# Retention front on one NeuronCore: eight units before the first layer, two tiles by turns on each weight, GpSimd given decays and low parts

## The chip, the cores and the metric

The kernel runs on one core of a Trainium2 chip. The metric is device microseconds of one execution; the median of three runs before the change is 1460.3 us (1460.2 to 1460.72).

## The reference

Retention with decay per head, then two gated or maximum feed-forward layers, all in float32:

```python
scores = scale * np.matmul(q, k.transpose(0, 1, 3, 2))          # 8 x 8 heads, 576 x 64
Dmat = np.where(rel >= 0, gamma[:, None, None] ** rel[None, :, :], 0.0)
attn = np.matmul(scores * Dmat[None, :, :, :], v)
x = attn.transpose(0, 2, 1, 3).reshape(B * S, H * D)            # 4608 x 512
h = np.maximum(np.maximum(x @ w1, x @ w2), x @ w3)              # 512 -> 768
x = h @ w_out                                                   # 768 -> 512
h = x @ w_in                                                    # 512 -> 2048
out = (h * np.clip(h + 3.0, 0.0, 6.0) / 6.0) @ w_out2           # 2048 -> 512
```

## The kernel before, in words

**Numbers.** TensorE multiplies in the fp32r type. Every operand of the feed-forward layers is kept as a high part (a cast on ScalarE) and a low part (the value minus the high part), and a product is three matmuls: high by high (L462), high by low (L463), low by high (L464). The weights come as float64 bits and are turned into floats on the core.

**A weight.** `Weights.step` is one conversion step for a 128x512 weight tile. On VectorE it runs L113 and L114 for the weight that begins, L132 and L134 for the one that joins and L154 (the low part) for the one that ends; on ScalarE L121, L124 and the cast L148; on GpSimd one product, L136. A weight passes through three steps. `fetch` loads the next weight tile (512 KB of int64) on SP's queue; three such tiles fit.

**A unit.** One unit is one batch and a pair of heads, 576 positions in nine chunks of 64. Its raw data is 1152 KB, loaded in two halves of 576 KB, first the two value parts (V), then the two others (Z). `prepare` multiplies the keys by decays (nine ScalarE instructions, L348). `keys` issues the sums of key times value (L356) and the scores (L277) on TensorE. `copied`, `mask` and `join` bring them back (ScalarE L368, VectorE L395 and L385). `values_mm` multiplies them (L313), `values_rest` scales the result (VectorE L411), and `finish` makes the high part of x on ScalarE (L326) and the low part on VectorE (L327). The ninth chunk has small instructions of its own (L405, L418).

**The order.** All is written out by hand (`manual_schedule`), and each engine runs its instructions in that order. The first eight units (batches 0 and 1, class `Summed`) stand in the front. In the first four the weight steps lie between the units' parts; in the last four there is also a `block` in each of two places. A block is `up` (12 matmuls of 512 columns) or `down` (12 as well) of tile 0 or 1. Eight blocks of tile 0 lie in the front so, and the list `plan` holds the next 39 of the two tiles. From `plan`'s end on, units of the next tile are computed between blocks (`visit`, `rest`, `ready`), and wherever TensorE has a block after that it has little else to wait for.

**Rooms.** Raw data of units sits in two pools of three tiles (`raw`, `rooms`): the seventh unit loaded takes the tile of the first. SP, the queue that issues nearly all transfers, uses eight semaphores in turn, so that a ninth transfer is not issued before the first has landed, and a transfer that has to wait for a tile holds back all that stand behind it in SP's order.

Of the kernel before, what the change touches and what calls it, by code (L numbers as in the profile page):

```python
# [7 lines left out]
F32 = mybir.dt.float32  # L8
# [8 lines left out]
P = 128  # L17
# [20 lines left out]
def retention_moe_moe2(ctx: ExitStack, tc, raw, w_a, w_b, factors, masks, out):  # L38
# [22 lines left out]
    xe_d = dram.tile([P, KM, TB], F32, name="xed")  # L61
    wq_d = [dram.tile([P, 7, 2, 2 * P], F32, name=f"wqd{j}") for j in range(F2 // 2)]
# [157 lines left out]
    order_a.insert(8, order_a.pop(6))  # L220
# [35 lines left out]
    xs, low = {}, []  # L256
    banks = [ps_at.tile([P, 512], F32, name=f"at{n}") for n in range(2)]

    class Unit:
# [63 lines left out]
        def finish(self, queue=late):  # L323
            b, hp, y = self.b, self.hp, self.y
            hi, lo = xs[b][:, 0, hp, :], xs[b][:, 1, hp, :]
            nc.scalar.copy(hi, y[:, :TB])  # L326
            queue.append(lambda: nc.vector.tensor_tensor(out=lo, in0=y[:, :TB], in1=f32(hi), op=ALU.subtract))  # L327
            late.append(lambda: nc.sync.dma_start(out=xe_d[:, hp, b * C:(b + 1) * C], in_=y[:, TB:]))
# [11 lines left out]
    class Summed(Unit):  # L340
# [3 lines left out]
        def prepare(self):  # L344
            h = (NC - 1) // 2
            for c in [*range(h, NC), *range(h)]:
                k = self.part(1, c, None, VS1)
                nc.scalar.mul(k, k, kdec_sb[:, self.hp, c:c + 1])  # L348

        def keys(self):  # L350
            h = (NC - 1) // 2
            for n, c in enumerate([*range(h, 2 * h), *range(h)]):
# [8 lines left out]
                self.scores(n, self.ps[0], n * C)  # L361
# [7 lines left out]

        def carry(self):  # L370
            t, h = raws[self.i], (NC - 1) // 2
            for e in (1, 0):
                own, other = halves[e], halves[1 - e]
                nc.tensor.matmul(
                    self.ps[1][other, h * C:].rearrange("p (n d) -> p n d", d=D), lhsT=same_sb[other, :],
                    rhs=self.part(e, h, VS0, VS1)[other, None, :].to_broadcast([D, h, D]),
                    start=False, stop=True, skip_group_check=True)
            self.copied(h)
# [19 lines left out]
        def values_mm(self):  # L398
            self.scores(NC - 1, self.ps[0], 0)
            self.values(range(NC - 1), self.ps[1])  # L400
            t = raws[self.i]
            for e in range(2):
                own, other = halves[e], halves[1 - e]
                z0 = (Z0, Z1)[e] + (NC - 1) * C
                nc.vector.scalar_tensor_tensor(  # L405
                    out=t[own, z0:z0 + C], in0=self.ps[0][other, :C], scalar=powers_sb[other, self.hp, 0, NC - 1:],
                    in1=mask_sb[other, self.hp], op0=ALU.mult, op1=ALU.mult)
# [546 lines left out]
```

## Time and profile before

| | |
|---|---|
| median of three runs | 1460.3 us |
| profiled execution: time, span | 1460.34 us, 1458.5 us |
| TensorE busy | 1442.5 us, 99% of the span |
| VectorE, ScalarE, GpSimd busy | 894.9, 458.2, 152.4 us |
| mean granted TensorE clock | 0.999 |
| HBM read, written | 174.42 MB, 42.99 MB |

Lines L12 are those of the kernel file. PE is TensorE, DVE VectorE, ACT ScalarE, POOL GpSimd, SP the queue that issues the transfers. A float32 matmul (L277, L313, L356) shows twice in the trace, once for each of its passes. The time is 1.84 us more than the span; that part lies around the execution and is taken as it is.

### The profile page before, as it was taken

What the parts mean: (1) busy time and instruction counts of PE and PEld (TensorE: products, weight loads), DVE (VectorE), ACT (ScalarE), POOL (GpSimd) and SP (SyncE); (2) the same over time, 40 slices, a digit from 0 to 9 for tenths busy, and PEclk for the clock granted to TensorE, in tenths of its full rate; (3) what the DMA queues carried; (4) which work ended last, traced back from release to release, by engine and by line L of the source; (5) the groups of instructions that cost most, each with busy time, mean ns of one, the idle gap of its engine ahead of it and who ended that gap; (6) DMA issues with size and microseconds to landing.
All of it is one profiled execution on the core that took longest, in us unless ns stands there. A gap on an engine that the chain in (4) does not pass through costs nothing.

```text
span 1458.5 us, 24565 instructions
## 1 busy us (share of the span) xinstructions
PE 1442.5 (99%) x9760; PEld 1248.3 (86%) x9760; DVE 894.9 (61%) x1867; ACT 458.2 (31%) x882; POOL 152.4 (10%) x116
## 2 busy tenths in 40 slices
PE   8999999999999999999999999999999999999998
PEld 7788888888888888888898899898898898898997
DVE  6997778777778752214446646555654655566544
ACT  7653233434343311112222322232232222223222
POOL 3332013333333300000000000000000000000000
PEclk9999999999999999999999999999999999999999
DMA  9543345656565501064643363364445436444431
GB/s 347 170 129 107 130 142 193 230 204 233 195 221 197 195 13 53 7 213 141 224 125 114 113 213 116 101 223 117 116 148 177 116 87 238 116 115 168 116 101 44
DMA packets 94499, 219.03 MB, mean 150 GB/s; under 512 B 14128, under 2 KB 17328, under 8 KB 94384
## 3 DMA queue, kind: packets, MB, share of 16 engines
q1 hardware_dynamic: 94016, 216.96, 45.3%
q8 instruction: 78, 1.28, 0.3%
q10 hardware_dynamic: 368, 0.48, 0.1%
q14 instruction: 37, 0.30, 0.1%
HBM read 174.42 MB, written 42.99 MB: 149 GB/s over the span
## 4 chain that ended last, share of the span: by engine, by line
PE 91%; DVE 7%; ACT 1%; DMA 1%; issue 1%; SPq 0%; ACTq 0%; DVEq 0%
PE mm L462 18%; PE mm L464 17%; PE mm L463 17%; PE o L795 5%; PE o L796 5%; PE o L794 5%; PE o L462 3%; PE o L463 3%; PE o L464 3%; PE p L796 3%; PE p L795 3%; PE p L794 3%; PE mm L313 2%; PE at L277 1%; DVE xf L685 1%
## 5 line engine op out<-in xcount | busy, mean ns | idle before, releaser
L53 ACT CAST gp<-g 128x384 fp32r<-128x384 f32 x192 | 98.6, 513 | 336.9 <-DVE g L751 331.9
L462 PE MATMUL mm<-x,w 128*128 128x512 f32 x468 | 185.2, 396 | 0.1
L464 PE MATMUL mm<-x,w 128*128 128x512 f32 x468 | 182.6, 390 | 0.0
L463 PE MATMUL mm<-x,w 128*128 128x512 f32 x468 | 182.5, 390 | 0.0
L54 DVE TENSOR_TENSOR gp<-g,gp 128x384 fp32r<-128x384 f32 x192 | 107.2, 558 | 112.2 <-ACT gp L53 112.2
L758 DVE TENSOR_TENSOR cc<-mm,c 128x384 f32<-128x384 f32 x142 | 78.7, 554 | 136.9 <-PE mm L464 95.4
L479 DVE TENSOR_TENSOR t<-mm,t 128x512 f32<-128x512 f32 x108 | 74.1, 686 | 135.4 <-PE mm L464 135.3
L795 PE MATMUL o<-w,gp 128*128 128x512 f32 x384 | 151.3, 394 | 0.0
L796 PE MATMUL o<-w,gp 128*128 128x512 f32 x384 | 150.7, 392 | 0.0
L794 PE MATMUL o<-w,gp 128*128 128x512 f32 x384 | 150.2, 391 | 0.0
L462 PE MATMUL mm<-T,wq 128*128 128x384 f32 x382 | 129.8, 340 | 0.9 <-ACT c L763 0.2
L763 ACT COPY c<-mm 128x384 f32<-128x384 f32 x143 | 68.5, 479 | 196.7 <-PE mm L464 196.7
L464 PE MATMUL mm<-T,wq 128*128 128x384 f32 x382 | 129.0, 338 | 0.0
L463 PE MATMUL mm<-T,wq 128*128 128x384 f32 x382 | 128.7, 337 | 0.0
L136 POOL TENSOR_TENSOR wf<-wf,wp 128x512 f32<-128x512 f32 x56 | 82.6, 1475 | 342.9 <-DVE wp L134 329.7
L462 PEld LDWEIGHTS mm<-x,w 128*128 128x128 f32 x468 | 87.9, 188 | 20.9 <-DVE wp L113 1.4
L464 PEld LDWEIGHTS mm<-x,w 128*128 128x128 f32 x468 | 87.9, 188 | 18.6
L463 PEld LDWEIGHTS mm<-x,w 128*128 128x128 f32 x468 | 88.0, 188 | 17.7
L53 ACT CAST h<-t 128x512 fp32r<-128x512 f32 x54 | 33.6, 622 | 204.6 <-DVE t L479 199.1
L462 PE MATMUL mm<-B,wq 128*128 128x384 f32 x286 | 96.5, 337 | 0.0
L464 PE MATMUL mm<-B,wq 128*128 128x384 f32 x286 | 96.4, 337 | 0.0
L463 PE MATMUL mm<-B,wq 128*128 128x384 f32 x286 | 96.2, 336 | 0.0
(177 smaller groups left out, 2923.1 us busy)
## 6 DMA issues: line engine op xcount, KB each, us to landing
wq<-wqd SPq DMA_DIRECT2D x336, 256.0 KB, 3.1
raw<-in_raw SPq DMA_DIRECT2D x55, 576.0 KB, 5.4
ws<-in_w_b SPq DMA_DIRECT2D x32, 512.0 KB, 4.6
ws<-in_w_a SPq DMA_DIRECT2D x24, 512.0 KB, 3.5
wqd<-y SPq DMA_DIRECT2D x24, 512.0 KB, 2.7
x2d<-y SPq DMA_DIRECT2D x18, 512.0 KB, 3.3
wod<-y SPq DMA_DIRECT2D x16, 512.0 KB, 3.0
w<-wod SPq DMA_DIRECT2D x16, 512.0 KB, 4.4
```

The costliest lines, as they stand in the source:

```text
L53: nc.scalar.copy(hi, full)
L54: late.append(lambda: nc.vector.tensor_tensor(out=lo, in0=full, in1=f32(hi), op=ALU.subtract))
L136: nc.gpsimd.tensor_tensor(out=frac, in0=frac, in1=f32(power), op=ALU.mult)
L462: nc.tensor.matmul(ps, lhsT=wh, rhs=xh, start=first, stop=False, skip_group_check=read)
L463: nc.tensor.matmul(ps, lhsT=wh, rhs=xl, start=False, stop=False, skip_group_check=read)
L464: nc.tensor.matmul(ps, lhsT=wl, rhs=xh, start=False, stop=last, skip_group_check=read)
L479: nc.vector.tensor_tensor(out=tmp[t, f], in0=ps, in1=tmp[t, f], op=ALU.max)
L758: nc.vector.tensor_tensor(out=c, in0=a, in1=b, op=ALU.add)
L763: nc.scalar.copy(c, ps)
L794: nc.tensor.matmul(outs[s], lhsT=gh, rhs=wo[f][:, 0, :], start=start, stop=False)
L795: nc.tensor.matmul(outs[s], lhsT=gh, rhs=wo[f][:, 1, :], start=False, stop=False)
L796: nc.tensor.matmul(outs[s], lhsT=gl, rhs=wo[f][:, 0, :], start=False, stop=stop)
```

## The change

- `prepare`: of units 2 to 7 one GpSimd instruction over all nine chunks (128x576). Units 0 and 1 keep ScalarE for five chunks and use one VectorE instruction for four.
- `finish`: the low part of x is made on GpSimd for seven of the eight front units, on VectorE for the last.
- The ninth chunk of the eight units is not computed in the front. `put_end` stores its four inputs (128 KB in pieces of 256 bytes) to HBM; class `Ends` loads all of them once (1 MB), and computes scores and values for the eight units behind two blocks of `plan`.
- The front holds the eight units, three conversion steps (behind units 2, 3 and 4) and one block, (0, 0, 0), behind unit 6. `carry` is gone: all units use `join`.
- `plan` holds the up blocks of tiles 0 and 1 by turns on each weight from the first weight on.
- Unit 5 is loaded before the table fills; weight tiles are fetched at other places, and unit 6 is loaded behind `put_end` of unit 0, unit 7 behind `put_end` of units 1 and 2.

```diff
-        def finish(self, queue=late):
+        def finish(self, eng=None):
             hi, lo = xs[b][:, 0, hp, :], xs[b][:, 1, hp, :]
             nc.scalar.copy(hi, y[:, :TB])
+            def rest(eng):
+                eng.tensor_tensor(out=lo, in0=y[:, :TB], in1=f32(hi), op=ALU.subtract)
+            if eng is not None:
+                rest(eng)
...
+            def scaled(eng, n):
+                eng.tensor_tensor(out=k[:, :n], in0=k[:, :n], in1=kdec_sb[:, self.hp, :n, None].to_broadcast([P, n, C]),
+                                  op=ALU.mult)
+            if self.i > 1:
+                scaled(nc.gpsimd, NC)
+                return
...
         def values_mm(self):
-            self.scores(NC - 1, self.ps[0], 0)
             self.values(range(NC - 1), self.ps[1])
...
+            self.finish(nc.vector if self.i == 2 * HP - 1 else nc.gpsimd)
+        def put_end(self):
+            t = raws[self.i].rearrange("p (k s) -> p k s", s=S)
+            nc.sync.dma_start(out=ends_d[:, self.b, self.hp], in_=t[:, :, TB:])
+    class Ends:
+        def load(self):
+            t = at.tile([P, RAW], F32, tag="raw", bufs=3, name="raw")[:, :2 * HP * 4 * C]
+            nc.sync.dma_start(out=t, in_=ends_d.rearrange("p b h k c -> p (b h k c)"))
...
+        def scores(self):
+            for b, hp in units[:2 * HP]:
+                for e in range(2):
+                    nc.tensor.matmul(ps[other, b, hp], lhsT=self.t[other, b, hp, 1 - e],
+                                     rhs=self.t[other, b, hp, e], start=True, stop=True)
...
         for i, u in enumerate(us):
             u.values_mm()
             if two:
                 two.keys()
                 two.copied(0)
             if three:
                 three.prepare()
             u.values_rest()
             if two:
                 two.mask()
+                two.join()
+            u.put_end()
+            if i == 0:
+                load_raw(6)
+                wa.fetch(1)
+            if i == 2:
+                load_raw(7, room())
+            if 1 < i < 5:
+                wa.step()
+            if i == 2 * HP - 2:
+                block(0, 0, 0)
+        ends = Ends()
+        load_raw(8)
+        load_raw(9)
+        ends.load()
...
-        plan = [(1, 0, j) for j in range(3)] + [(0, 0), (0, 2, 2)] + [(1, 1, j) for j in range(3)] + [(0, 1)]
+        plan = []
+        for f in range(F1 - 1):
             for j in range(3):
                 plan += [(0, f, j), (1, f, j)]
+            if f:
+                plan.append((0, f - 1))
```

SP's queue in the front. `raw` and `room` are units' data (from the top units 0, 1, 2, 3, 4, 5, 6, 7), `ws` weight tiles, `xed` and `endsd` the HBM tiles of the ninth chunks. Before:

```order
L238 DMA room_150<-in_raw 128x1152 x2
L100 DMA ws_153<-in_w_a 128x512
L238 DMA raw_395<-in_raw 128x1152 x2
L328 DMA xed_75<-yr_385 128x64
L100 DMA ws_428<-in_w_a 128x512
L238 DMA raw_483<-in_raw 128x1152 x2
L328 DMA xed_75<-yr_473 128x64
L100 DMA ws_518<-in_w_a 128x512
L238 DMA room_572<-in_raw 128x1152 x2
```

After, at the same place:

```order
L238 DMA room_149<-in_raw 128x1152 x2
L101 DMA ws_152<-in_w_a 128x512
L238 DMA raw_154<-in_raw 128x1152 x2
L419 DMA endsd_76<-raw_134 128x4x64
L238 DMA raw_364<-in_raw 128x1152 x2
L101 DMA ws_367<-in_w_a 128x512
L419 DMA endsd_76<-raw_138 128x4x64
L419 DMA endsd_76<-room_141 128x4x64
L238 DMA room_489<-in_raw 128x1152 x2
```

Unit 6 (`raw_364`) takes the tile of unit 0 (`raw_134`), which the store just ahead of it reads, and unit 7 (`room_489`) takes the tile of unit 2 (`room_141`), again read by the store just ahead; before, nothing read those tiles so late. One weight tile fewer stands ahead of unit 5.

VectorE at the end of the front: `yr` is a unit's scaled result, `x` its low part, `t` the maximum of two up blocks. Before, the last unit's end:

```order
L411 TENSOR_TENSOR yr_1046<-at1_122,w_126 128x512
L418 SCALAR_TENSOR_TENSOR yr_1046<-at0_121,factors_sb_119,masks_sb_120 128x64
L327 TENSOR_TENSOR x_166<-yr_751,x_166 128x512
L327 TENSOR_TENSOR x_166<-yr_875,x_166 128x512
L327 TENSOR_TENSOR x_166<-yr_971,x_166 128x512
L327 TENSOR_TENSOR x_166<-yr_1046,x_166 128x512
L479 TENSOR_TENSOR t_1061<-mm_1072,t_1061 128x512
```

After (`w_772` is the second weight):

```order
L413 TENSOR_TENSOR yr_754<-at1_123,w_127 128x512
L329 TENSOR_TENSOR x_168<-yr_754,x_168 128x512
L114 TENSOR_SCALAR wp_774<-ws_567 128x512
L115 TENSOR_SCALAR wf_775<-ws_567 128x512
L133 SCALAR_TENSOR_TENSOR wf_632<-ws_367,wf_632 128x512
L135 SCALAR_TENSOR_TENSOR wp_631<-ws_367,wp_631 128x512
L155 TENSOR_TENSOR w_772<-wf_559,w_772 128x512
```

The low part of the second weight is now made behind the last unit's end and four instructions of a conversion step; before, eight weights were ready at this place.

## Rows read from the trace of the kernel before

**Rows 1.** The page: busy time, share of the span and instructions of each engine.

```profile
PE 1442.5 (99%) x9760; PEld 1248.3 (86%) x9760; DVE 894.9 (61%) x1867; ACT 458.2 (31%) x882; POOL 152.4 (10%) x116
```

**Rows 2.** Stretch 70 to 140: length, busy of each engine, granted clock, DMA, GB/s.

```profile
70.00:140.00 70.00, 70.00 (x310) 57.99 (x309) 62.54 (x100) 34.25 (x59) 23.84 (x15) 1.00 0.38 123
```

**Rows 3.** TensorE's waits from 60 to 160: total, times, longest.

```profile
PE at L313 <- DVE room L405: 0.5, 1, 0.5
```

**Rows 4.** TensorE in order of time: start, duration, line, tiles, shape; 61 to 68.

```profile
61.98 0.39 PE L464 MATMUL mm<-x,w 128*128 128x512 f32 x1
...
62.56 1.15 PE L313 MATMUL at<-room 128*64 128x64 f32 x32
63.64 0.50 PE L462 MATMUL mm<-x,w 128*128 128x512 f32 x1
63.98 0.40 PE L463 MATMUL mm<-x,w 128*128 128x512 f32 x1
...
67.38 0.50 PE L462 MATMUL mm<-x,w 128*128 128x512 f32 x1
```

**Rows 5.** TensorE, the last matmul of the 29th block from 67.38 on.

```profile
146.19 0.39 PE L464 MATMUL mm<-x,v 128*128 128x512 f32 x1
```

**Rows 6.** DMA issues from 15.0 to 19.7: count, KB, us to landing.

```profile
raw<-in_raw SPq DMA_DIRECT2D x1, 576.0 KB, 11.4
xed<-yr SPq DMA_DIRECT2D x1, 32.0 KB, 6.9
```

**Rows 7.** SP's queue in order of time: start, issuing time, transfer.

```profile
13.76 1.61 SPq L238 DMA_DIRECT2D raw<-in_raw  x2
19.66 0.33 SPq L328 DMA_DIRECT2D xed<-yr  x1
...
28.41 1.57 SPq L238 DMA_DIRECT2D room<-in_raw  x2
```

**Rows 8.** DMA issues from 51.8 to 52.3 (issued at 51.87 and 52.25).

```profile
raw<-in_raw SPq DMA_DIRECT2D x1, 576.0 KB, 4.5
ws<-in_w_a SPq DMA_DIRECT2D x1, 512.0 KB, 3.5
```

**Rows 9.** GpSimd in order of time: the table fills, and one product beside VectorE.

```profile
5.72 8.06 POOL L335 TENSOR_TENSOR w<-masks_sb,factors_sb 128x512 f32<-128x512 f32 x8 [5.28 <-DMA masks_sb<-in_masks]
...
28.03 1.67 POOL L136 TENSOR_TENSOR wf<-wf,wp 128x512 f32<-128x512 f32 x1 [4.41 <-DVE wp L134]
```

**Rows 10.** TensorE, a unit's keys and scores: its first and its last row.

```profile
13.85 0.43 PE L356 MATMUL o<-room 64*64 64x256 f32 x2
...
15.96 0.28 PE L356 MATMUL o<-room 64*64 64x64 f32 x4
```

**Rows 11.** TensorE, one up block's first matmul and what follows its last.

```profile
37.01 0.50 PE L462 MATMUL mm<-x,w 128*128 128x512 f32 x1
...
39.96 0.34 PE L313 MATMUL at<-room 128*64 128x64 f32 x4
```

**Rows 12.** TensorE, one of three idle times with no releaser (the others 1.03, 1.13).

```profile
19.85 0.43 PE L356 MATMUL mm<-room 64*64 64x256 f32 x2 [1.33 <-issue]
```

**Rows 13.** TensorE's last matmul.

```profile
1452.13 0.39 PE L796 MATMUL p<-w,gp 128*128 128x512 f32 x1
```

**Rows 14.** Stretch 1455 to 1456, columns as in rows 2.

```profile
1455.00:1456.00 1.00, 0.00 (x0) 0.00 (x0) 0.00 (x0) 0.00 (x0) 0.00 (x0) 0.50 0.95 248
```

**Rows 15.** VectorE in order of time: a scaled result, four low parts, a conversion step.

```profile
28.46 0.68 DVE L411 TENSOR_TENSOR yr<-o,w 128x512 f32<-128x512 f32 x1
...
33.88 2.49 DVE L327 TENSOR_TENSOR x<-yr,x 128x512 fp32r<-128x512 f32 x4
36.28 0.42 DVE L113 TENSOR_SCALAR wp<-ws 128x512 uint32<-128x512 uint32 x1
...
38.16 0.69 DVE L154 TENSOR_TENSOR w<-wf,w 128x512 fp32r<-128x512 f32 x1
```

**Rows 16.** ScalarE, the cast to a unit's high part.

```profile
19.60 0.61 ACT L326 CAST x<-yr 128x512 fp32r<-128x512 f32 x1
```

More of the change, by code (lines that the diff above doesn't have):

```diff
@@ L345, in prepare, with keys @@
             h = (NC - 1) // 2
[L346 to L350, printed above, removed]
+            k = raws[self.i][:, VS1:VS0].rearrange("p (c s) -> p c s", s=C)
+            def scaled(eng, n):
[4 more added lines that the diff above has]
+                return
+            for c in range(h, NC):
+                nc.scalar.mul(k[:, c], k[:, c], kdec_sb[:, self.hp, c:c + 1])
+            scaled(nc.vector, h)
+        def keys(self, apart=False):
             h = (NC - 1) // 2
@@ L360, in keys @@
                         start=(c == h), stop=(c == h - 1), skip_group_check=True)
-                self.scores(n, self.ps[0], n * C)
+                if not apart:
+                    self.scores(n, self.ps[0], n * C)
+            if apart:
+                for n in range(2 * h):
+                    self.scores(n, self.ps[0], n * C)
         def copied(self, c):
@@ L368, in copied @@
                 nc.scalar.copy(t[other, v0:v0 + n], self.ps[1][other, c * C:c * C + n])
[L370 to L378, printed above, removed]
         def join(self):
@@ L518, in retention_moe_moe2 @@
         load_raw(2, room())
-        wa.fetch(1)
         load_raw(3, room())
@@ L523, in retention_moe_moe2 @@
         wa.fetch(1)
+        load_raw(5)
         nc.vector.memset(rebias, -896.0)
@@ L536, in retention_moe_moe2 @@
         us[0].prepare()
-        us[0].keys()
+        us[0].keys(apart=True)
+        us[0].copied(0)
         us[1].prepare()
-        us[0].copied(0)
         us[0].mask()
@@ L558, in block @@
                 up(t, f, j)
-        early = [(0, f, j) for f in range(3) for j in range(3)][:8]
         for i, u in enumerate(us):
-            one, two, three = (us[i + n] if i + n < len(us) else None for n in (1, 2, 3))
+            two, three = (us[i + n] if i + n < len(us) else None for n in (2, 3))
             u.values_mm()
-            flush()
-            if 0 < i < HP - 1 or HP <= i < 2 * HP - 1:
-                wa.step()
-            if one and one.i >= HP:
-                one.carry()
             if two:
@@ L613, in retention_moe_moe2 @@
         decay(2 * HP)
-        base = 2 * HP
-        side = {(1, f, 0): [(visit, 0)], (0, f, 1): [(ready, 0)], (1, f, 1): [(rest, 0)]}
+        base, skipped = 2 * HP, ((1, 3, 2), (1, 4, 2))
+        side = {(1, 3, 2): [(lambda k: ends.scores(), 0)], (1, 4, 2): [(lambda k: ends.values(), 0)],
+                (1, f, 0): [(visit, 0)], (0, f, 1): [(ready, 0)], (1, f, 1): [(rest, 0)]}
         for n, (a, b) in enumerate(zip([(0, f - 1), (1, f, 2), (1, 1), (1, 3)], [(0, f), (1, 0), (1, 2), (1, 4)])):
@@ L619, in retention_moe_moe2 @@
         for n, blk in enumerate(plan):
-            block(*blk)
-            if wa.ended < NA and (n % 3 or not n):
+            if n:
+                block(*blk)
+            if wa.ended < NA and (n % 3 or not n) and blk not in skipped:
                 wa.step()
```

75 lines of the change are left out of this document (30 added, 45 removed).

## Prediction

> **What bounds the kernel now.** I read the page first: TensorE is busy for 99% of the span [rows 1], so only a stretch in which TensorE has no blocks yet can give anything back. From 70 to 140 TensorE is busy throughout while VectorE is at 89% [rows 2], and from 60 to 160 it waits once, for 0.5 us [rows 3]. So the front ends where the eighth block of tile 0 starts, at 67.38 [rows 4]; from there to the 29th block's end there is no gap worth naming: 146.42 (146.19 plus one pitch of 0.23) less 67.38 is 79.04 us, 2.73 us a block [rows 4, 5]. Seven blocks are behind TensorE at 67.38.
>
> In the changed kernel TensorE has one block behind it, (0, 0, 0), when its unbroken run begins with block (1, 0, 0), at a time that I call B. Six more blocks than before lie behind that point, 6 x 2.73 = 16.4 us. The whole question is how early B comes, and what is lost behind it. Everything later is the same work in the same order, so what the front gains or loses is the change of the time.
>
> **What leaves VectorE.** Of the conversion steps, 2.6 us each (36.28 to the end at 38.85 [rows 15]), which made eight weights in the front, three remain; seven low parts of 0.6 (2.49 for four [rows 15]), and the ninth chunk's instructions go as well. VectorE ceases to be the bound there. But then B is set by what arrives last, and that is unit 7's data, by way of SP's queue.
>
> **SP's queue, the term that decides.** Before, the second half of unit 5 is issued at about 15.0 (the second of the pair that starts at 13.76 [rows 7]) and lands 11.4 later [rows 6], at 26.4. A half costs 1.4 us of the queue once it flows (52.25 + 4.5 against 51.87 + 3.5 [rows 8]), so a weight tile costs 1.2. One tile fewer stands ahead of unit 5 now: 25.2. The store of unit 0's ninth chunk stands behind it. The row for such a store: issued at 19.66 behind unit 5, it landed 6.9 later at 26.56 [rows 6, 7], 0.2 behind the read ahead of it. Stores wait their turn behind reads. The new one is four times as large in pieces of the same size: 0.2 to 0.8, I take 0.5, so 25.7. Only then is unit 6's load issued, since it overwrites what the store reads, and the queue has run empty. From an empty queue a 512 KB tile needs 3.5 [rows 8], a half 3.7: 29.4, the second half 30.8, the weight tile 32.0, two stores of 0.5 each 33.0. Unit 7's load waits for the second of these: 33.0 + 3.7 = 36.7, second half 38.1. Before, it was issued at 28.41 [rows 7]. So the stores empty the queue twice, and this eats most of what VectorE gives.
>
> **From unit 7's data to B.** GpSimd scales the keys: a fill of 512 columns takes 1.0 (8.06 for eight), a product beside VectorE 1.67 [rows 9]; for 576 columns that is 1.1 to 1.9, I take 1.4: 36.7 + 1.4 = 38.1, when the second half is there too. Then on TensorE, from 38.2: keys and scores 2.4 (13.85 to 16.24 [rows 10]), unit 6's values 1.1 (62.56 to 63.64 [rows 4]), the block (0, 0, 0) with its switch 2.95 [rows 11], unit 7's values 1.1: 7.55, so 45.75. Two more terms. First, TensorE stood three times for 1.0 to 1.3 us in runs of small matmuls with no releaser [rows 12]; such a stop between 38 and 46 costs 0 to 1.3, I take 0.5. (The Trainium skill, Runtime: NRT & Kernel Launch, Instruction fetch mechanics, calls the cost of refilling instructions mostly hidden; by that this term would be 0 and the time 0.5 us earlier.) Second, the clock: TensorE ends unit 5's values at about 34.4 (30.8 for scaled keys of unit 6, 2.4, 1.1) and has nothing until 38.2, 3.8 us. Its last matmul in the trace begins at 1452.13 [rows 13], and from 1455 to 1456 the granted clock is 0.50, 1.2 GHz [rows 14]. So after a wait as long as this the clock has fallen in this very trace. No row has matmuls at that level: keys and values of 3.5 us would cost nothing more at least and double at most, so 0 to 3.5; I take 1.7, the middle. (The Trainium skill, TensorE: Matmul & The Clock Gate, Part 1, says that an idle array falls to 1.2 GHz and returns to 2.4 only after sustained work; by that the term is nearer its upper end, and the time at most 1.8 us later than I say. The fall in the rows agrees; how the clock returns no row here shows.) **B is 45.75 + 0.5 + 1.7 = 47.95.**
>
> **Behind B.** The block (1, 0, 0) reads unit 7's part of x last, and that is there in time. The next, (0, 0, 1), needs the second weight's low part in its third matmul, 3.3 us behind B (14 matmuls of 0.23). VectorE gets to that only behind unit 7: result 0.1 + 0.7, cast 0.65 [rows 16], low part 0.65, and a step of 2.6 [rows 15]: 4.7. A stop of 1.4. A little later the step for the sixth weight waits for its tile, whose fetch stands on SP behind the load of the stored ends, which waits for unit 7's store; it holds VectorE's maximum of block (1, 0, 1) and by that a PSUM buffer: I take 0.3, between 0 and 1.0. The ends themselves: 32 passes for scores and 32 for values, in two places between blocks. Unit 6's 36 passes between two blocks cost 1.55 (61.98 to 63.98, less two pitches [rows 4]); 64-row scores run partly side by side, so at most 3.1 for both and at least 1.6; I take 2.4. In the front this work was under VectorE's time and cost nothing.
>
> **What costs nothing.** The casts of x stay. Low parts and decays on GpSimd, seven and six instructions of 1.0 to 1.9, need at most 25 us between 14 and 46, and only unit 7's decay is on the path. Conversion behind B needs 2.6 us of VectorE for each weight, and a weight now feeds two blocks, 5.5 us; with maxima and low parts it stays under TensorE, as it did at 89% [rows 2]. Were that cover gone, every weight would add its excess. Unit 10 now loads into unit 8's tile instead of unit 6's and so waits for unit 8's values; it has two blocks and a visit, over 7 us, against 3.7 + 1.4 [rows 8], so I cost it at nothing, and at one or two us if SP is late. The four `carry` products go, under the same waits.
>
> **Sum.** 47.95 + 1.4 + 0.3 + 2.4 + 16.4 = 68.45 against 67.38: 1.1 us later. The profiled execution took 1460.34, 0.04 above the median; 1460.34 + 1.1 = **1461.4**. A difference under 0.2% (2.9 us) is one that a measurement of this kernel can't tell from none.
>
> **Rivals.**
> *Stores don't hold up loads (faster).* If the store of unit 0 lands long before unit 5's data, unit 6 follows at once (28.0), the tile (29.2), unit 7 (32.0), and TensorE's own units become the limit: from about 6, when the table fills have begun [rows 9], 8 x 3.5 + 2.95 + about 3 for first waits end at 40, with the fall of the clock gone too. 40 + 20.5 = 60.5: 6.9 us gained, 1453.5. Against it speaks the xed row. With the stores at their cheap end (0.2 each), no fall of the clock and no stop, B is 44.9 and the loss behind it a little smaller: about 3.3 gained, 1457. Together 0.16.
> *The clock stays low (slower).* If TensorE comes out of its wait at 1.2 GHz and stays there through keys, values and the first block, 6.5 us count double: 4.8 more than I took, 1466. For it speaks that the wait is longer than the one in rows 13 and 14; against it, that the mean granted clock of the execution is 0.999 (the table), though TensorE stood for 1.3 us at a time in the front [rows 12]. It decides from 1.9 us more than the 1.7 taken, on top of the 1.1. Chance 0.27.
> *The change does not do what it says:* VectorE and GpSimd block each other so far that weights come late behind B for several blocks, and TensorE stops about 1 us at each of the first three or four: 1465, in the same class, 0.04 of its own.
>
> **How the numbers follow.** Forecast, within 0.2%: 0.53. Faster by more: 0.16. Slower by more: 0.27 + 0.04 = 0.31. The unknown costs give, from the sum, downwards 0.9 (three stores), 1.7, 0.5, 0.8 (ends), 0.5 (stops behind B), and upwards 0.9, 0.5 (GpSimd), 1.8, 0.8, 0.7, 1.3; they won't all fall on one side, and of the slower rival a part must be inside. I take 1457.3 to 1465.0, which leaves out the first faster rival and the far end of the slower one.
>
> **What will show it.** Right: SP's load of unit 6 issued only at 25 to 26.5, that of unit 7 at 32 to 34, with two holes in DMA's share there; TensorE idle for some 3 us or more ahead of unit 7's keys; a granted clock under 1.00 around 38 to 43; block (1, 0, 0) at 46 to 50, a stop of 1 to 2 us in (0, 0, 1), then none until tile 2. Wrong: unit 6 issued before 20, or block (1, 0, 0) before 43 (then faster), or stops on weights at more than two blocks behind B (then slower).

## The result, and the profile after

The changed kernel takes 1469.1 us (median of four runs, 1467.3 to 1473.3) against 1460.5 for the kernel before: 1.0060 times as long, 95% interval 1.0036 to 1.0084, some 8.6 us slower. The profiled execution took 1467.27 with a span of 1465.5, 6.9 more than the profiled one before. Against the same instructions of the kernel before, the stores of tile 0's result near 163 us are 6.9 late, and the last output rows 6.6. So the loss is made in the front and just behind it, and the rest is as it was. One run of a later kernel, e_step5 (1900.3 us at a mean granted clock of 0.704), is left out of its median.

TensorE's busy time and share, as in [rows 1]:

```profile
PE 1444.0 (99%) x9744; PEld 1251.4 (85%) x9744; DVE 895.3 (61%) x1858; ACT 440.7 (30%) x812; POOL 168.2 (11%) x129
```

SP's queue, as in [rows 7]: start, issuing time, transfer.

```profile
15.64 0.38 SPq L419 DMA_DIRECT2D endsd<-raw  x1
25.73 0.81 SPq L238 DMA_DIRECT2D raw<-in_raw  x2
26.58 1.45 SPq L101 DMA_DIRECT2D ws<-in_w_a  x1
28.14 0.38 SPq L419 DMA_DIRECT2D endsd<-raw  x1
28.62 0.45 SPq L419 DMA_DIRECT2D endsd<-room  x1
35.51 0.82 SPq L238 DMA_DIRECT2D room<-in_raw  x2
...
50.94 0.33 SPq L428 DMA_DIRECT2D raw<-endsd  x1
55.56 0.33 SPq L101 DMA_DIRECT2D ws<-in_w_a  x1
```

The store of unit 0 goes out at 15.64, and unit 6's load, which takes the same tile, only at 25.73; unit 7's follows the third store by 6.9 us. The store at 28.62 itself (DMA issues from 28.6 to 28.7: KB, us to landing):

```profile
endsd<-room SPq DMA_DIRECT2D x1, 128.0 KB, 6.8
```

So it landed at 35.4, 0.1 before unit 7's load; the weight tile ahead of it had landed at 33.2 and the store before it at 33.7. The packets show what this last store waited for: a 16 KB transfer of instructions runs from 33.38 to 34.34, all else was through at 33.8, and from 34.33 on the store's last small packets follow one by one (DMA from 33.3 to 34.4, its instruction queue; DMA from 34.3 to 34.8):

```profile
q8 instruction: 1, 0.02, 5.5%
```
```profile
DMA packets 16, 0.00 MB, mean 8 GB/s; under 512 B 16, under 2 KB 16, under 8 KB 16
```

That these packets stood behind the instructions on one and the same DMA engine is read from the times; the trace does not name a packet's engine. What TensorE makes of the late load, in order of time (columns as in [rows 4]):

```profile
31.40 0.43 PE L372 MATMUL o<-raw 64*64 64x256 f32 x2 [0.93 <-POOL raw L356]
...
33.73 1.15 PE L313 MATMUL o<-raw 128*64 128x64 f32 x32
41.17 0.69 PE L372 MATMUL at<-room 64*64 64x256 f32 x2 [6.29 <-POOL room L356]
...
45.64 1.86 PE L313 MATMUL o<-raw 128*64 128x64 f32 x32
47.43 0.50 PE L502 MATMUL mm<-x,w 128*128 128x512 f32 x1
...
50.39 1.15 PE L313 MATMUL at<-room 128*64 128x64 f32 x32
51.48 0.50 PE L502 MATMUL mm<-x,w 128*128 128x512 f32 x1
...
56.19 0.50 PE L504 MATMUL mm<-x,w 128*128 128x512 f32 x1 [1.17 <-DVE w L155]
...
65.83 0.50 PE L502 MATMUL mm<-x,w 128*128 128x512 f32 x1 [1.63 <-DVE t L519]
```

Unit 6's keys and scores take 2.33 us (31.40 to 33.73), unit 7's, behind the wait, 4.47 (41.17 to 45.64); values take 1.09 (50.39 to 51.48) or 1.79 (45.64 to 47.43). The stretches tell why (length, busy of PE, PEld, DVE, ACT, POOL, granted clock, DMA share, GB/s):

```profile
35.00:40.00 5.00, 0.00 (x0) 0.00 (x0) 4.89 (x10) 2.71 (x5) 1.36 (x2) 0.70 0.69 219
40.00:45.00 5.00, 3.83 (x56) 3.11 (x60) 0.71 (x2) 0.00 (x0) 3.60 (x3) 0.50 1.04 334
45.00:50.00 5.00, 5.00 (x57) 4.38 (x54) 2.82 (x5) 1.87 (x4) 1.85 (x2) 0.78 0.24 41
```

TensorE stands, the clock falls to 0.50 (1.2 GHz) and stays there through unit 7's keys and unit 6's values. The prediction's point B, the start of block (1, 0, 0), is 51.48. Two stops stand behind it. The second (2.02 from the matmul before, so 1.79 beyond the pitch of 0.23) has its cause on VectorE, which waits for a weight's transfer:

```profile
62.60 0.43 DVE L114 TENSOR_SCALAR wp<-ws 128x512 uint32<-128x512 uint32 x1 [2.29 <-DMA ws<-in_w_a]
```

That tile's load is issued at 55.56, when the step before has freed its buffer, and lands at 62.5. The loads of units 8 and 9 and of the stored ends (1 MB, issued at 50.94, landed at 61.2) run ahead of it in the queue (DMA issues at 50.94 and at 55.56: KB, us to landing):

```profile
raw<-endsd SPq DMA_DIRECT2D x1, 1024.0 KB, 10.3
```
```profile
ws<-in_w_a SPq DMA_DIRECT2D x1, 512.0 KB, 6.9
```

### The profile page after: what moved, and what is told of

Read it like the earlier page. It is cut to its first block, busy times and chain, and to the rows that moved or that the text cites. A ratio compares the mean times of both kernels' runs of the same rounds, so it can differ in the third digit from the quotient of the medians.

```text
span 1465.5 us, 24497 instructions
## 1 busy us (share of the span) xinstructions
PE 1444.0 (99%) x9744; PEld 1251.4 (85%) x9744; DVE 895.3 (61%) x1858; ACT 440.7 (30%) x812; POOL 168.2 (11%) x129
## 4 chain that ended last, share of the span: by engine, by line
PE 90%; DVE 5%; DMA 2%; ACT 1%; POOL 1%; issue 0%; ACTq 0%; POOLq 0%; SPq 0%; DVEq 0%
PE mm L502 17%; PE mm L504 17%; PE mm L503 17%; PE o L822 5%; PE o L823 5%; PE o L821 5%; PE o L502 3%; PE o L504 3%; PE o L503 3%; PE p L823 3%; PE p L822 3%; PE p L821 3%; PE mm L313 2%; PE at L277 1%; DVE xf L712 1%; DVE g L778 1%
## 5 line engine op out<-in xcount | busy, mean ns | idle before, releaser
L53 ACT CAST h<-t 128x512 fp32r<-128x512 f32 x54 | 33.6, 622 | 204.5 <-DVE t L519 192.2
```

The source lines that it names most:

```text
L53: nc.scalar.copy(hi, full)
```

## Experiments

Three explanations stood against each other. **Theory 1:** loads that wait for stores bring TensorE's wait, and that brings the low clock; what stands in queues ahead of weights brings the stops behind the front. **Theory 2:** GpSimd's new work, or VectorE beside it, is the slow link. **Theory 3:** weights can't come faster, so an earlier front gains nothing. In the profiled execution all of the loss but the ends' two passes stands ahead of 70 us, so B and the stops behind it (the excess over the pitch) are read from each kernel's profiled execution, beside the medians. A profiled execution can lie 2 us to either side of its kernel's median, hence both.

| kernel | B, us | stops over 0.3 behind B, us | median, us | times the kernel before (95%) |
|---|---|---|---|---|
| changed | 51.48 | 1.34, 1.79 | 1469.1 | 1.0060 (1.0036 to 1.0084) |
| e_warm | 49.27 | 0.93, 0.37, 1.41, 1.77 | 1466.7 | 1.0035 (1.0022 to 1.0048) |
| e_ends_late | 51.37 | 1.40, 0.34, 3.19, 0.36 | 1470.3 | 1.0060 (1.0048 to 1.0073) |
| e_ends16 | 51.67 | 0.33, 0.98, 0.40, 1.76 | 1467.1 | 1.0042 (1.0028 to 1.0056) |
| e_decay | 50.93 | 1.41, 2.25 | 1469.3 | 1.0057 (1.0044 to 1.0069) |
| e_small | 51.74 | 1.39 | 1466.4 | 1.0044 (1.0032 to 1.0057) |
| e_step5 | no trace | no trace | 1473.2 | 1.0083 (1.0069 to 1.0097) |
| e_step5_decay | 51.17 | 1.02, 0.52, 5.68, 0.37 | 1473.5 | 1.0087 (1.0073 to 1.0100) |
| e_gp | 58.80 | 0.38, 1.97, slow clock | 1476.5 | 1.0112 (1.0096 to 1.0127) |
| e_rooms | 45.15 | 3.82 | 1464.2 | 1.0021 (1.0011 to 1.0030) |
| e_all | 46.49 | 1.41, 2.37 | 1465.4 | 1.0028 (1.0018 to 1.0039) |
| e_noends | 47.42 | 1.40, 0.39, 1.76 | 1459.5 | 0.9988 (0.9980 to 0.9997) |
| e_best | 46.16 | 1.06, 1.14, 0.50, 0.67 | 1462.5 | 1.0011 (1.0002 to 1.0020) |
| e_best2 | 45.47 | 0.86, 1.47 | 1460.3 | 0.9999 (0.9990 to 1.0007) |
| e_best3 | 48.13 | 0.82 | 1460.1 | 0.9994 (0.9986 to 1.0003) |
| e_best4 | 45.45 | 0.89, 0.73 | 1460.8 | 0.9997 (0.9988 to 1.0006) |

(For e_best2 to 4, B is the first block behind unit 7's values. The ends' two passes, 1.17 us each, are left out of the stops.) The profiled executions of e_warm, e_best2 and e_best4 show no fall of the clock in the front or behind it, each of the others one to three.

**e_warm: work for TensorE while it waits.**

```diff
+            if i == 5:
+                for n in range(36):
+                    nc.tensor.matmul(pairs[3][0][halves[n % 2], :256].rearrange("p (n d) -> p n d", d=C),
+                                     lhsT=zeros[halves[n % 2], :],
+                                     rhs=zeros[halves[n % 2], None, :].to_broadcast([C, 4, C]), start=True, stop=True)
             if two:
                 two.keys()
```

> The changed kernel with 36 more matmuls on zeros, 64x256 each, into an accumulator bank that is free there, ahead of unit 7's keys: TensorE has something to do in the 6.3 us in which it waits for unit 7. Nothing else is touched. Theory 1 (TensorE's wait lets the clock fall to 1.2 GHz, and the small matmuls behind it pay): the granted clock stays at 1.00 from 36 to 47 us, unit 7's keys go from 4.47 to about 2.35 us and unit 6's values from 1.79 to 1.1, block (1,0,0) starts at 48.6 instead of 51.5, and the time is 2.8 us shorter. Theory 2 (these two are slow for another reason, such as data or code that comes in late): the durations stay, block (1,0,0) at 51.5, no change.

The stretches, and TensorE behind unit 7's keys:

```profile
35.00:40.00 5.00, 5.00 (x50) 3.25 (x48) 4.92 (x10) 2.29 (x4) 0.61 (x2) 1.00 0.62 191
40.00:45.00 5.00, 5.00 (x118) 4.05 (x116) 0.86 (x2) 0.67 (x3) 3.53 (x3) 1.00 1.07 344
```
```profile
44.15 1.15 PE L313 MATMUL o<-raw 128*64 128x64 f32 x32
45.23 0.50 PE L502 MATMUL mm<-x,w 128*128 128x512 f32 x1
```

The clock stays at 1.00, unit 6's values take 1.08 instead of 1.79, and B comes 2.2 earlier although unit 7's load went out 0.5 later. So the low clock is a cost, and of this size, at B. In the time less of it is seen. The median falls by 2.4, but the two intervals overlap, and the profiled execution is only 0.6 shorter: its stops are 1.35 longer in all, with a new one of 1.77 at 114 us (last section).

**e_ends_late, e_ends16: what weight 5 stands behind.** The first moves three loads behind the eleventh block, and unit 8's decay with them; the second moves only the load of the ends, behind the 17th.

```diff
-        load_raw(8)
-        load_raw(9)
-        ends.load()
...
+            if n == 10:
+                load_raw(8)
+                load_raw(9)
+                ends.load()
+                decay(2 * HP)
```

> The changed kernel with the loads of units 8 and 9 and the load of the last chunks issued after the eleventh block instead of ahead of the second. Theory 1 (the stop of 1.8 us at 63.8 us is weight 5's transfer, which stands on the queue behind those loads): the stop falls under 0.3 us, weight 5's load is issued near 52 instead of 55.6, and the time is 1.6 to 1.9 us shorter. Theory 2 (VectorE's three steps for one weight are what is late there): the stop stays over 1 us and the time does not change by over 0.5 us. Block (1,0,0) starts at 51.5 by both.

The stop at 63.8 is gone, but three loads in a row stand ahead of another weight, VectorE waits for it 35 us later, and the clock falls again (100.4 to 103.9). The time is no shorter. VectorE there:

```profile
97.52 0.43 DVE L114 TENSOR_SCALAR wp<-ws 128x512 uint32<-128x512 uint32 x1 [3.45 <-DMA ws<-in_w_a]
```

> The changed kernel with the load of the last chunks alone issued later, after block 17 (units 8 and 9 stay where they are). Theory 1 (weight 5 is late at 63.8 us because its load stands on SP's queue behind that load, which waits for unit 7's store): weight 5 is issued near 51 instead of 55.6 us, the stop of 1.8 us falls under 0.5 us, no new one comes, and the time is 1.3 to 1.8 us shorter. Theory 3 (the weights' chain on VectorE and ScalarE is what is late): the stop stays over 1 us, and the time is within 0.5 us of the changed kernel.

The stop falls from 1.79 to 0.40, though weight 5's load is issued no sooner (55.77): it lands 4.9 later instead of 6.9. So the tile waits in the transfers' queue, not on SP, where I had put it. The median falls by 2.1, with intervals that overlap; the profiled execution is 0.7 longer, with a new stop of 1.76 at 114.3, whose cause is told in the last section.

This trace shows a second link on the way to B. Unit 7's load goes out at 34.44, 1.1 sooner than in the changed kernel, and still its keys begin at 41.48, 0.3 later: the decay on GpSimd, 1.42 there, takes 2.71 here, beside a conversion step on VectorE.

```profile
38.71 2.71 POOL L356 TENSOR_TENSOR room<-room,factors_sb 128x576 f32<-128x576 f32 x1 [2.35 <-DMA room<-in_raw]
```

It takes 2.88 in e_ends_late and 2.35 in e_step5_decay, where that load is some 0.5 early. So a load that is early by an us or less gains nothing, and theory 2 has a part in TensorE's wait.

**e_rooms: five buffers, so that no load waits for a store.** `hyp` holds the hidden values' tiles and is opened where `rooms` closes.

```diff
-        return rooms.tile([P, RAW], F32, tag="room", bufs=3, name="room")
+        return rooms.tile([P, RAW], F32, tag="room", bufs=5, name="room")
...
         load_raw(5)
+        load_raw(6, room())
+        wa.fetch(1)
+        load_raw(7, room())
...
         v_pool = tc.alloc_tile_pool(name="v", bufs=1, reuse_waits="tile")
+        hyp.append(tc.alloc_tile_pool(name="hyp", bufs=1, reuse_waits="tile"))
```

> The changed kernel with five buffers instead of three for the units' inputs on the left side (the tiles of the hidden values take that place later), so that units 6 and 7 are loaded right behind unit 5 and no load waits for a store of last chunks. All else is as in the changed kernel. Theory 1 (the loads that wait for stores are the cause): unit 7 lands by 33 us, TensorE's wait of 6.3 us goes, the clock stays at 1.00 from 20 us on, block (1,0,0) starts at 43 to 45 us, bound by VectorE's order (about 7 us earlier), and the time is 6 to 8 us shorter: level with the kernel before. Theory 2 (GpSimd's decays and low parts, or VectorE beside them, are the slow link): the wait only moves, block (1,0,0) starts at 48 or later, and less than 3 us come back. Theory 3 (the order behind the front costs the time): the front ends as early as by theory 1, but TensorE stops longer behind it, and less than 3 us come back.

B moves from 51.48 to 45.15, close to what theory 1 has, but only 4.9 us of the median come back. The clock did not stay at 1.00: it was at 0.50 from 32.6 to 36.0, behind a stop of 1.93 us at 31.15 for which the trace has no releaser, and from 53.1 to 56.5, behind the stop shown next. TensorE's stop behind B, and ScalarE, which ends it:

```profile
51.85 0.50 PE L502 MATMUL mm<-x,w 128*128 128x512 f32 x1 [3.65 <-ACT w L149]
```
```profile
50.51 0.77 ACT L254 ACTIVATE raw<-raw,factors_sb 128x576 f32<-128x576 f32 x1 [3.90 <-DMA raw<-in_raw]
51.19 0.60 ACT L149 CAST w<-wf 128x512 fp32r<-128x512 f32 x1
```

Unit 8's decay (L254) stands in ScalarE's order ahead of weight 1's high part (L149) and waits for unit 8's load. With the front as late as in the changed kernel that load was there in time; with an earlier front it is not. A new wait took the place of the old one.

**e_all: e_rooms and e_ends_late together.**

> The five buffers and the later loads of units 8, 9 and the last chunks together. Theory 1: the two add up, block (1,0,0) at 43 to 45 us and no stop of over 0.3 us near 56 to 58 us; 8 to 10 us shorter than the changed kernel, which is 0 to 2 us under the kernel before. Theory 2 or 3: at most 4 us shorter than the changed kernel.

They don't add up: the decay's wait is gone (1.41 where 3.82 stood), but the three loads in a row bring 2.37 and a fall of the clock from 96.2 to 99.6, as alone.

**e_gp: GpSimd's new work taken away.**

```diff
-            if self.i > 1:
-                scaled(nc.gpsimd, NC)
-                return
-            for c in range(h, NC):
+            for c in [*range(h, NC), *range(h)] if self.i > 1 else range(h, NC):
                 nc.scalar.mul(k[:, c], k[:, c], kdec_sb[:, self.hp, c:c + 1])
-            scaled(nc.vector, h)
+            if self.i <= 1:
+                scaled(nc.vector, h)
...
-            self.finish(nc.vector if self.i == 2 * HP - 1 else nc.gpsimd)
+            self.finish(nc.vector)
```

> The changed kernel with units 2 to 7's decays back on ScalarE (nine products each) and the low parts on VectorE; GpSimd keeps the tables and the weights' products. Theory 1 (GpSimd's work is not on the path, the loads are): unit 7 is issued at 35 to 36 us again, block (1,0,0) starts at 51 to 52.5 us, and the time stays within 1 us of the changed kernel. Theory 2 (the decays and low parts on GpSimd hold the keys or slow VectorE): TensorE's waits for decays, 0.9 and 2.1 us, go, block (1,0,0) starts 2 us or more earlier, and the time is 2 us or more shorter.

Neither: 7.4 slower than the changed kernel. TensorE's longest waits from 14 to 60 (total, times, longest), and VectorE:

```profile
PE at L313 <- DVE room L393: 4.5, 2, 2.7
PE o L313 <- DVE room L393: 2.7, 1, 2.7
```
```profile
31.75 0.69 DVE L329 TENSOR_TENSOR x<-yr,x 128x512 fp32r<-128x512 f32 x1 [3.50 <-ACT x L326]
```

The cast (L326) now stands on ScalarE behind nine decays of the next unit, and VectorE's low part waits for it with a mask and a sum behind it. The clock was at 0.50 from 36.6 to 50.3 besides. So this edit prices an order, and the waits and the low clock that it brings, not GpSimd alone. The gain that theory 2 forecast did not come; what GpSimd's work costs by itself this run can't tell.

**e_before_gp: that part alone, in the kernel before** (`prepare` as in the change; low parts of the first eight units on GpSimd).

> The kernel before with one part of the change alone: the decays as in the changed kernel (units 0 and 1 on ScalarE and VectorE, the others one product on GpSimd) and the low parts of the first eight units on GpSimd right behind their high parts. Theory 1: no gain and no loss over 1 us, since what ends TensorE's waits in this front is data and weights. Theory 2: slower than the kernel before by 2 us or more, with TensorE waiting for GpSimd's products.

1463.2, 1.0013 times the kernel before (1.0004 to 1.0022): 2.6 us slower, more than theory 1 allowed and what theory 2 asked for. Its first blocks come up to 0.5 later, and a stop at 58.1 grows from 1.24 to 3.01. VectorE there, and GpSimd:

```profile
56.18 1.79 DVE L134 SCALAR_TENSOR_TENSOR wp<-ws,wp 128x512 uint32<-128x512 uint32 x1
...
58.49 1.75 DVE L54 TENSOR_TENSOR h<-t,h 128x512 fp32r<-128x512 f32 x1
```
```profile
56.05 1.36 POOL L328 TENSOR_TENSOR x<-yr,x 128x512 fp32r<-128x512 f32 x1 [2.85 <-ACT x L326]
58.11 1.58 POOL L136 TENSOR_TENSOR wf<-wf,wp 128x512 f32<-128x512 f32 x1 [0.70 <-DVE wp L134]
```

Both VectorE operations take 0.69 elsewhere; each loses 1.1 beside a GpSimd instruction. Behind that stop the clock is at 0.50 from 60.8 to 64.2, and a block takes 4.29 instead of 2.95. So theory 2 has a true core, worth 1.8 us of stop in the order of before, where VectorE is on the path at 58 us, and 1.3 more by the low clock behind it.

**e_noends: the changed kernel without the last chunks** (no store, load or matmul of them; zeros are written).

> The changed kernel without the last chunks of the first eight units: nothing of them is stored, loaded or computed, and zeros are written in their place. Theory 1: unit 6's load is issued near 15 us and unit 7's near 25 us, TensorE's 6.3 us wait goes, block (1,0,0) starts at 44 to 46 us; the stop of 1.8 us at 63.8 us (weight 5 behind the load of last chunks) and the 2.3 us of the last chunks' matmuls go too; 9 to 11 us shorter than the changed kernel, if nothing new stops TensorE. Theory 2: unit 7's keys still wait for GpSimd by 3 us or more, and block (1,0,0) starts at 48 or later.

9.6 under the changed kernel: the last chunks, computed later, cost all of the loss. B came later than expected, at 47.42, since unit 7's decay stood on GpSimd behind a weight's product that waits for VectorE: TensorE waited 2.1 for it and had, behind that, a low clock from 39.5 to 42.9.

**e_best, e_best2: what follows from these.** The first takes e_rooms, spreads the later loads and unit 8's decay over the plan, and adds a conversion step in the front (the fourth there; the text below counts it as the third). The shares of the three are not separated.

```diff
-            if 1 < i < 5:
+            if 1 < i < 6:
                 wa.step()
...
+        later = {4: lambda: load_raw(8), 10: lambda: load_raw(9), 16: ends.load, 22: lambda: decay(2 * HP)}
...
+            if n in later:
+                later[n]()
```

> Five buffers for the units' inputs (units 6 and 7 loaded right behind unit 5); a third conversion step for weights in the front (after unit 5, where VectorE is idle for 5.1 us in the changed kernel); and behind the front the loads of unit 8, unit 9 and the last chunks, and unit 8's decay on ScalarE, spread over the plan (after blocks 5, 11, 17 and 23). Theory 1 (late loads, the cold clock that they bring, and what stands in queues ahead of weights 1 and 5 are the whole loss): block (1,0,0) starts near 45 us as with the five buffers alone, the stops behind it fall from 3.8 and 0.3 us to under 0.5 us in all, and the time is 9 to 10 us under the changed kernel, 0 to 3 us under the kernel before. Theory 3 (weights can't come faster behind an earlier front): a stop of 2 us or more stands again between 45 and 110 us, and at most 6 us come back.

6.6 under the changed kernel, not 9 to 10. The long stops are gone; what is left waits for unit 7's output (TensorE behind B):

```profile
48.71 0.51 PE L502 MATMUL mm<-x,w 128*128 128x512 f32 x1 [0.89 <-ACT x L326]
...
50.08 0.50 PE L503 MATMUL mm<-x,w 128*128 128x512 f32 x1 [0.86 <-POOL x L329]
```

and from 31.4 to 47.3 VectorE is the bound (15.61 of 15.90 us busy):

```profile
31.40:47.30 15.90, 12.92 (x263) 11.02 (x263) 15.61 (x28) 8.86 (x17) 8.29 (x7) 1.00 0.36 102
```

```diff
-            if three:
+            if three and i != 4:
                 three.prepare()
...
-            if 1 < i < 6:
+            if i == 3:
+                us[7].prepare()
+            if i in (1, 2, 3, 5):
                 wa.step()
...
+        plan[1], plan[2] = plan[2], plan[1]
```

> The version with five buffers and spread loads, further: conversion steps for weights after units 1, 2, 3 and 5 instead of 2 to 5, so that VectorE's mask and sum for unit 7 don't stand behind one; unit 7's decay on GpSimd ahead of a weight's product instead of behind it; and tile 0's second block before tile 1's first, since the latter needs unit 7's output, 3 us behind its matmuls. Theory 1 (VectorE's order is the next bound once the loads are early): the first block after unit 7's values starts at 44 to 45 instead of 46.2 us, the stops of 1.1 and 1.1 us behind it go, and the time is 3 to 4 us under the version before it: 0.5 to 2 us under the kernel before. Theory 3 (weights are the bound): stops of 2 us or more in all stand between 45 and 70 us, and less than 1.5 us come back.

2.3 under e_best, and level with the kernel before. **e_best3 and e_best4** leave out single conversion steps behind the front (`n not in (2,)`, `n not in (1, 4)`).

> The last version (five buffers, spread loads, conversion steps after units 1, 2, 3 and 5, tile 0's second block first) with the conversion step behind block 3 left to a later block, so that VectorE's maximum, which frees TensorE's accumulator, does not stand behind it. Theory 1 (VectorE's order makes the stops of 0.9 and 1.5 us at 50.8 and 57.4 us): one of the two goes, and the time is 0.8 to 1.5 us under that version, which is 0.1 to 0.2% under the kernel before. Theory 3 (the weights themselves are late): a stop as long comes within the next three blocks, and the time stays within 0.5 us.

> The same with the steps behind blocks 2 and 5 left out instead. Theory 1: both stops shrink, 1 to 2 us under that version. Theory 3: a weight is late by 1.5 us or more near 60 to 75 us, no change or slower.

In both the stop of 1.47 goes and no weight is late for it, so it was VectorE's order; but neither gains what was expected, the times stay within some 0.5 us. In e_best3's profiled execution the clock fell at 33.6 to 40.4 and B was 2.7 later; such falls are as large as what is left to gain.

**Three small edits, and one that went wrong.**

> The changed kernel with one more conversion step for weights in the front, after unit 5, where VectorE is idle from 40.7 to 45.8 us while unit 7 is awaited. Theory 1 (the stop of 1.3 us in the second block behind the front is VectorE's order: weight 1's low part stands behind unit 7's and two other weights' work): block (1,0,0) still starts at 51.5 us, the stop falls under 0.4 us, and the time is 0.9 to 1.4 us shorter. Theory 3 (weights 1 to 5 can't come faster): the stop moves to a later block, and the time is within 0.5 us of the changed kernel.

1473.2 (1.0083, 1.0069 to 1.0097), 4 us slower than the changed kernel (the next text says 5, from a median with the run left out here). That VectorE is idle from 40.7 to 45.8 was no room for this step: in VectorE's order it stands behind unit 7's mask, so behind the wait. This is read from the order alone. With the decay moved as well:

> A third conversion step in the front and unit 8's decay moved behind block 23. The third step alone made the changed kernel 5 us slower. If that loss came from the decay (unit 8's load goes out after the fifth weight's, so the decay waits until 57 us and weight 1 behind it), the time is 4 us or more under that kernel, at 1468 to 1470 us. If it came from VectorE (the step stands behind unit 7's mask, ahead of the outputs of units 6 and 7), it stays over 1472 us, and block (1,0,0) stops for units 6 and 7.

1473.5: it stays slow, so not the decay; nor, mainly, units 6 and 7 (1.0 of stops). SP's queue, VectorE and TensorE:

```profile
56.61 0.33 SPq L428 DMA_DIRECT2D raw<-endsd  x1
```
```profile
66.44 0.43 DVE L114 TENSOR_SCALAR wp<-ws 128x512 uint32<-128x512 uint32 x1 [5.38 <-DMA ws<-in_w_a]
```
```profile
69.67 0.80 PE L502 MATMUL mm<-x,w 128*128 128x512 f32 x1 [5.52 <-DVE t L519]
```

The step's own fetch waits on SP for VectorE (issued at 50.66), and unit 7's store and the loads of units 8, 9 and the ends stand behind it. The ends' load goes out at 56.6 instead of 50.9, right ahead of the next weight's, which lands 9.3 after its issue. The second stop grew from 1.79 to 5.68, and the clock fell behind it. Neither answer that I had offered was the right one.

```diff
-        decay(2 * HP)
...
+            if n == 22:
+                decay(2 * HP)
```

> The changed kernel with unit 8's decay alone moved on ScalarE: after block 23 instead of ahead of the plan. In the five-buffer kernel it waited 3.9 us for unit 8's load, with weight 1's high part queued behind it; in the changed kernel's profiled run it did not wait. If it is part of this kernel's loss too, the time is 0.3 to 2 us shorter and the stop of 1.3 us in the second block behind the front falls by 0.3 us or more; if not, within 0.5 us.

No change. The profiled execution does show one way in which this front gets slower: the clock falls again behind the second stop.

```profile
66.10:69.40 3.30, 3.30 (x9) 2.62 (x8) 3.28 (x7) 2.29 (x4) 1.22 (x2) 0.50 0.43 129
```

> Three edits of the changed kernel that leave its buffers alone: zero matmuls in TensorE's wait for unit 7 (2.4 us shorter alone), the load of the last chunks after block 17 (2.1 us shorter alone), unit 8's decay after block 23. If the losses add up, block (1,0,0) starts at 49 us and the time is 4 to 5.5 us under the changed kernel, at 1463.5 to 1465 us; if the second stop only covers what the cold clock left, 1466 to 1467 us.

1466.4, no better than the zero matmuls alone. The second stop is gone (the median does not show it), but here the clock fell behind an earlier wait, unit 6's of 2.15 us, so that unit 6's keys took 4.4, and the zeros then held TensorE to 44.3 though unit 7's decay had ended at 42.35.

```profile
32.60:36.00 3.40, 3.40 (x60) 2.97 (x60) 2.59 (x4) 0.76 (x2) 1.77 (x2) 0.50 0.51 142
```

## Why the prediction was wrong, step by step

Ahead of B the mechanism was the predicted one; behind it, one of two stops came another way. Three sizes were too small, all on the same side.

- **Unit 6's load at 25.7:** 25.73. The store of unit 0 landed 9.9 after its issue, right behind unit 5's data.
- **"29.4, the second half 30.8, the weight tile 32.0, two stores of 0.5 each 33.0":** this is the first step that failed. Unit 7's load went out at 35.51. From 25.73 to the weight tile's landing the reads took 7.5, not 6.3. The first store took 0.5, as predicted, the second 1.6; the 1.1 above the prediction is about the length of the instruction transfer shown above (0.96). In the seven other traces with this order of the queue the two stores took 0.8 to 0.9 together (1.6 in one), so their size was right; the reads took 7.5 to 9.4, and unit 7's load went out at 34.2 to 36.8, never at 33.0. So the term that was too small in every run is that of the reads behind an emptied queue, taken from [rows 8], where little else ran. Why they take so much longer, and so unevenly, stays open. With its first half landing 4.0 after its issue (3.7 predicted) and 1.42 on GpSimd (1.4 predicted, at most 1.9; three other traces have 2.4 to 2.9), unit 7's keys began at 41.17, 3.0 later than predicted.
- **Stop 0.5 and clock 1.7:** no stop of TensorE's sequencer was seen there; the clock cost 2.84 (4.47 less 2.33, 1.79 less 1.09), so 0.6 more than the two terms. It was inside the bounds given, 0 to 3.5. The Trainium skill's sentence (TensorE: Matmul & The Clock Gate, Part 1) that the full clock returns only after sustained work agrees with these rows: matmuls began at 41.17, and the clock was at 0.50 until 47.2.
- **B at 47.95:** 51.48, 3.5 later: 3.0 by the load, 0.6 by the clock. Block and values (2.95, 1.1) took 2.96 and 1.09.
- **Stop of 1.4 in (0, 0, 1):** 1.34, with the releaser named. Right.
- **"I take 0.3, between 0 and 1.0"** for the weight behind the load of the ends: 1.79. The second step that failed. The transfer ahead of it was the right one, the way not: the weight's fetch goes out as soon as its own buffer is free, and it then has 3.4 MB of loads (units 8 and 9, the ends) ahead of it in the queue, which unit 7's store lets out only from 48.1 on. I had counted the time to issue, not these transfers.
- **Ends 2.4:** two passes of 1.17 beyond the pitch, with the switches 2.6. Right.
- **Sum:** 51.48 + 1.34 + 1.79 + 2.6 + 16.4 and some 0.6 of small gaps is 74.2, against 68.45: 5.8 more, 3.5 of it ahead of B and 2.3 behind it.

**The range** failed by one sentence: "they won't all fall on one side". They did, and the first two hang together: a later load of unit 7 makes TensorE's wait longer, and in all five traces in which TensorE had nothing to do in that wait (4.9 to 6.3 us) the clock fell. For the second stop behind B no such tie is shown: in e_warm, with a full clock and B 2.2 earlier, 1.41 of it stayed. All upward bounds together were 6.0; that end, 1467.4, was the profiled execution's time. The median lies 1.8 above that. Of the three other runs one, 1473.27, has a lower mean clock (0.993 against 0.995); the others, 1468.3 and 1469.93, have not (0.996, 0.995), and what makes them slower stays open.

**The rivals.** "The clock stays low" (1466, 0.27) was nearest: the clock was low through keys and values, but up again at the block, and the late load came on top. "Stores don't hold up loads" priced a case that e_rooms made real, at 1453.5; its median is 1464.2. That price took TensorE as the next limit, as did the sentence that VectorE ceases to be the bound. In e_best VectorE is busy for 98% from 31 to 47. "VectorE and GpSimd block each other" is a real cost (e_before_gp, and unit 7's decay in e_ends16), but not what makes most of this loss: without the last chunks, and with GpSimd's work as it is, all of it is gone (e_noends).

**Where the expected gain went.** The shorter work of the front became a wait for data that stores had put off; with the loads early, B comes 6 us sooner and meets the next bounds (VectorE's order, ScalarE's decay), and with these handled the change is level with the kernel before: 0.9994 to 0.9999. No version was shown to be faster with the last chunks computed; without them it is 0.1% faster (e_noends). Open is how much of the low parts' and decays' move is gain: e_gp's edit brought a wait of its own. Open is also what TensorE's stops without a releaser cost in the kernels whose loads come early: 1.5 to 1.9 us at 31 to 32 us in each of them, as in [rows 12], and 1.8 more at 38 us in e_best2 and e_best4. No run takes them away.

## What to carry to other kernels

A store out of a buffer that the next load needs is a wait on the whole queue ahead of it: take the load's start from when that store lands behind all reads issued before it, not from the store's size, and give those reads a range: from an emptied queue they took 7.5 to 9.4 us here, where the pace of two single transfers gave 6.3. When one late transfer feeds several unknowns, add their upper ends instead of letting them cancel. And before an early transfer is priced as a gain, look one engine on for what is queued behind an instruction that waits on the next transfer (here a decay on ScalarE ahead of a weight).

## What the chip showed beyond this

**The clock can fall after work has begun again.** In the changed kernel TensorE stood from 13.1 to 15.1; the clock was still full at the start of the next work and fell in its midst. The values behind it took 1.8 too, not 1.1.

```profile
13.10:15.10 2.00, 0.00 (x0) 0.00 (x0) 1.88 (x4) 0.00 (x0) 1.98 (x2) 1.00 1.03 414
15.20:16.40 1.20, 1.20 (x41) 1.10 (x44) 0.00 (x0) 0.00 (x0) 0.78 (x1) 1.00 1.06 417
16.60:19.80 3.20, 3.20 (x54) 2.81 (x50) 1.25 (x2) 1.25 (x3) 0.20 (x2) 0.50 1.01 408
```

The same wait of 2 us stands in e_warm without a fall. So a wait of this length costs TensorE nothing in one run and 2 us in another. In the changed kernel these 2 us don't reach B, since unit 7's data comes later still.

**VectorE and GpSimd take turns, and either may lose.** The same pair of instructions near 111 us: VectorE's and GpSimd's in the changed kernel, then GpSimd's in e_ends16.

```profile
111.62 1.52 DVE L114 TENSOR_SCALAR wp<-ws 128x512 uint32<-128x512 uint32 x1
```
```profile
111.25 1.61 POOL L137 TENSOR_TENSOR wf<-wf,wp 128x512 f32<-128x512 f32 x1 [4.54 <-DVE wp L135]
```
```profile
110.52 3.48 POOL L137 TENSOR_TENSOR wf<-wf,wp 128x512 f32<-128x512 f32 x1 [4.55 <-DVE wp L135]
```

In the changed kernel VectorE takes 1.52 instead of 0.42. In e_ends16 GpSimd takes 3.48 instead of 1.61 while VectorE runs through five instructions at its own pace; the weight is late, and TensorE stops for 1.76. The stops of 1.77 in e_warm and 1.76 in e_noends have the same row behind them (3.49 and 3.48 on GpSimd). The Trainium skill (SBUF — State Buffer, Who interferes with whom) says of a VectorE instruction that uses both port pairs that the one that issues first holds the shared pair for its whole instruction and the other waits; VectorE's row agrees, since it ends 0.28 after GpSimd's.
